# Windowed attention with sinks, then a multiplicative FFN: two megabytes of weights uncast by SyncE, sink scores in column tiles, sink values by small DMAs

## The chip, the cores and the metric

The kernel runs on one core of one Trainium2 chip. The metric is the device time of one execution in microseconds (us). Kernels that are compared ran in turn on the same chip. A run counts as slow when it is over 1.5% above the fastest of the same kernel; 10 of the 47 runs of the kernel before beside e1 to e15, and two of e11, are slow. The medians below are of all runs, the ratios of the fast ones alone. Engine names are those of the profile: PE is TensorE, PEld its weight loads, DVE VectorE, ACT ScalarE, POOL GpSimd, SP SyncE; "SPq" marks what SyncE's queue issues. L-numbers are lines of the kernel that was profiled, so the same statement has other numbers in another kernel.

The kernel before is itself uneven. In 18 of those 47 runs its mean granted clock was 0.983 to 0.991, and these took 210.04 us or more; the other 29 (0.995 to 1.000) took 207.32 to 210.10 us. The profiled run is one of the latter, so no trace shows where the clock falls in the former.

A ratio below is the mean time of one kernel's fast runs over the mean of the other kernel's fast runs of the same rounds. It is therefore not quite the ratio of the medians that stand beside it.

## The reference, cut to what matters

```python
def _attn_ref(q, k, v, n_sink, window):       # B, H, S, D = 4, 8, 768, 64; n_sink 4, window 128
    scores = scale * np.matmul(q, k.transpose(0, 1, 3, 2))
    keep = is_sink | in_window                # the first 4 keys, or the last 128
    scores = np.where(keep, scores, -1000000000.0)
    a = softmax(scores)                       # [cut: written out with max, exp and sum]
    return np.matmul(a, v)

def _moe_ref(x, w1, w2, w3, w_out):           # 3072 tokens, d_model 512, d_ff 1024
    h = (x @ w1) * (x @ w2) @ w3
    return h @ w_out
```

## The kernel before

1. **The order of instructions is planned when the kernel is built.** A small list scheduler inside the kernel holds tasks with guessed stage times. It simulates PE, ACT, DVE and SP and emits each engine's instructions in the order that this simulation gives. On the chip each engine follows its list in order, however the true times fall.
2. **Loads** of q, k, v and most weights are cast from float32 to bfloat16 on the way, by DMAs that GpSimd issues. The first half of w_out (1 MB) comes uncast by SyncE and is cast by ScalarE.
3. **w3 and w_out are folded** into w3 x w_out at the start, while q, k and v arrive.
4. **Batches 2 and 3 get their q and k transposed by DMA**, issued by SyncE: 12 a batch. SyncE also issues the 24 output stores.
5. **The output buffer** `o_sb` has three copies. ScalarE fills one from PSUM, SyncE stores it, and only then may ScalarE fill it again.

```python
    work = ctx.enter_context(tc.tile_pool(name="work", bufs=3))
    ps_mm = ctx.enter_context(tc.tile_pool(name="ps_mm", bufs=4, space=PSUM))
    # ...
    def transposes_dma(src, dst, kb):                     # batches 2 and 3
        nc.sync.dma_start_transpose(out=dst[:, :, kb * P:(kb + 1) * P], in_=src[:, kb, :])
        yield
    # ...
    def sink_values(b):                                   # 8 matmuls and a copy
        vp = ps_mm.tile([P, H, D], FP32, tag="mm", name="vp")
        for h in range(H):
            nc.tensor.matmul(vp[:, h, :], sel[:, h, :], vN[b][:, 0, h, 0:D],
                             start=(h == 0), stop=(h == H - 1))
        yield
        nc.scalar.copy(vs[b][:, :, 0:D], vp[:])
        yield

    def sink_scores(b, t):                                # 4 full-width matmuls, summed
        sp = ps_mm.tile([P, 256], FP32, tag="mm", name="sp")
        for r in range(NP):
            nc.tensor.matmul(sp[:], ksbd[b][:, r * P:(r + 1) * P],
                             qT[b][:, r, t * 256:(t + 1) * 256],
                             start=(r == 0), stop=(r == NP - 1))
        yield
        nc.scalar.activation(es[b][:, (t - 1) * 256:t * 256], sp[:], ACTF.Exp, scale=scale)
        yield
    # ...
    def project(b, m):
        po = ps_mm.tile([P, DM], FP32, tag="mm", name="po")
        # ... 8 matmuls
        yield
        o_sb = work.tile([P, DM], FP32, tag="o_sb", name="o_sb")      # 3 buffers
        nc.scalar.copy(o_sb[:], po[:])
        yield
        nc.sync.dma_start(out=out[t0:t0 + P, :], in_=o_sb[:])
        yield
```

The softmax here doesn't subtract the row's maximum and nothing guards it: scores larger than these inputs give would overflow.

## Time and profile before

| | before |
|---|---|
| median of the first 3 runs | 208.65 us (207.53 to 210.79) |
| span of the profiled run | 207.3 us |
| PE busy | 196.6 us, 95% |
| filler matmuls ("pz", meant only to keep PE's clock up) | 8.66 us, all before 15 us |
| longest wait of PE after the start | 2.51 us, ending at 94.58 us |

The page of the kernel before: the busy line, then three rows of the picture in 40 slices of 5.2 us (busy tenths of PE and ACT, granted PE clock in tenths; 9 is 90% or more).

```profile
PE 196.6 (95%) x1841; PEld 124.6 (60%) x1853; DVE 109.9 (53%) x262; ACT 112.6 (54%) x191; POOL 75.5 (36%) x98
PE   7999799999999999977999999999999999999992
ACT  4204567637657876665686766677654333333331
PEclk9999999999999999999999999999999999999999
```

PE is full nearly everywhere, so PE time is what counts. The dip in the middle is one wait. In the timeline of PE before, the columns are start and length in us, engine, line, operation, operands and count; the bracket gives the idle time ahead and what ended it.

```profile
94.58 0.41 PE L207 MATMUL vp<-vN_93,sel 128*128 128x64 bf16 x8 [2.51 <-DMA vN_93<-in_v_dram]
97.25 1.05 PE L217 MATMUL sp<-qT_96,ksbd_112 128*128 128x256 bf16 x8
98.13 0.39 PE L284 MATMUL xt<-ident,xn 128*128 128x128 bf16 x4
```

The first line is the wait: PE's list has the sink values of batch 3 next, and their v has not landed. The second line is two groups of sink scores. From 97.25 to the next start at 98.13 they take 0.88 us of the stream, 0.44 us a group.

Timeline of SP before, in the stretch where batch 2 is transposed:

```profile
61.74 0.36 SPq L352 DMA_DIRECT2D out_dram<-o_sb  x1
63.09 1.30 SPq L192 DMA_TRANSPOSE kT_100<-kN_88  x1
64.50 1.98 SPq L192 DMA_TRANSPOSE qT_96<-qN_84  x1
66.53 1.29 SPq L192 DMA_TRANSPOSE kT_100<-kN_88  x1
67.87 0.59 SPq L352 DMA_DIRECT2D out_dram<-o_sb  x1
68.51 1.26 SPq L192 DMA_TRANSPOSE qT_96<-qN_84  x1
...
87.20 1.32 SPq L192 DMA_TRANSPOSE qT_96<-qN_84  x1
```

SyncE counts as idle on a page, as issuing is not busy time. But from 63.1 to 69.8 us its queue has no gap to speak of: each transpose holds it for 1.2 to 2 us, and lands about 8.1 us after its issue.

### The profile page before, as it was taken

How to read it: one execution, taken by the hardware profiler on the slowest of the kernel's cores; microseconds unless marked ns; L12 is line 12 of the kernel's file. 1: busy time of each engine (PE TensorE's matmuls, PEld its weight loads, DVE VectorE, ACT ScalarE, POOL GpSimd, SP SyncE). 2: the span in 40 equal slices, each digit the busy share in tenths (PEclk: the TensorE clock that was granted, in tenths of full speed). 3: DMA queues.
4: the chain of work that ended last, by engine and by line, in shares of the span. 5: the costliest groups of instructions: out<-in, count | busy, mean ns of one | idle time of the engine just before them, and what ended most of it. 6: DMA issues, size and time to landing. Idle time of an engine off the chain costs nothing.

```text
span 207.3 us, 4572 instructions
## 1 busy us (share of the span) xinstructions
PE 196.6 (95%) x1841; PEld 124.6 (60%) x1853; DVE 109.9 (53%) x262; ACT 112.6 (54%) x191; POOL 75.5 (36%) x98
## 2 busy tenths in 40 slices
PE   7999799999999999977999999999999999999992
PEld 2454566797877875645666666666655566654440
DVE  7223586865887684574777757677751144430000
ACT  4204567637657876665686766677654333333331
POOL 7859784499999636652910000000000000000000
PEclk9999999999999999999999999999999999999999
DMA  6999999999999999999999930000004300003332
GB/s 213 152 209 161 182 175 207 185 157 154 155 155 183 137 161 155 127 210 184 145 134 124 153 118 0 5 0 3 0 0 155 152 0 2 3 0 153 151 152 102
DMA packets 96245, 24.94 MB, mean 120 GB/s; under 512 B 88544, under 2 KB 92128, under 8 KB 96224
## 3 DMA queue, kind: packets, MB, share of 16 engines
q0 software_dynamic: 79168, 14.16, 89.9%
q1 hardware_dynamic: 17056, 10.49, 24.3%
q8 instruction: 14, 0.23, 0.5%
q14 instruction: 7, 0.06, 0.1%
HBM read 29.36 MB, written 6.29 MB: 172 GB/s over the span
## 4 chain that ended last, share of the span: by engine, by line
PE 52%; DMA 27%; POOL 16%; issue 3%; ACT 0%; POOLq 0%; ACTq 0%
PE pg L299 27%; PE po L345 16%; DMA w_sb<-in_moe_w_dram 15%; DMA vN_93<-in_v_dram 7%; DMA qN_84<-in_q_dram 6%; PE av L268 4%; PE sc L237 3%; POOL qN_83 L103 3%; POOL vN_91 L103 2%; POOL kN_87 L103 2%; PE xt L284 2%; POOL w_sb L110 1%; POOL qN_84 L103 1%; POOL vN_92 L103 1%; POOL kN_88 L103 1%
## 5 line engine op out<-in xcount | busy, mean ns | idle before, releaser
L299 PEld LDWEIGHTS <-w_sb 128*128 128x128 bf16 x576 | 53.0, 98 | 24.8 <-issue 1.4
L242 ACT ACTIVATE ex<-sc 128x1024 bf16<-128x1024 f32 (+1 forms) x48 | 45.3, 958 | 7.9 <-PE sc L237 6.7
L306 ACT COPY a_sb<-pg 128x384 f32<-128x384 f32 (+1 forms) x72 | 32.0, 445 | 31.9 <-PE pg L299 17.4
L246 DVE TENSOR_TENSOR am<-ex,maskt 128x1024 bf16<-128x1024 bf16 (+1 forms) x48 | 30.3, 642 | 5.5 <-ACT ex L242 5.1
L349 ACT COPY o_sb<-po 128x512 f32<-128x512 f32 x24 | 14.0, 585 | 26.3 <-PE po L345 25.3
L299 PE MATMUL pg<-xT_102,w_sb 128*128 128x256 bf16 x192 | 24.7, 273 | 0.5 <-DMA w_sb<-in_moe_w_dram 0.5
L299 PE MATMUL pg<-xT_103,w_sb 128*128 128x384 bf16 x128 | 23.6, 326 | 0.0
L299 PE MATMUL pg<-xT_104,w_sb 128*128 128x384 bf16 x128 | 23.4, 326 | 0.0
L274 DVE TENSOR_TENSOR xn<-av,rec 128x256 bf16<-128x256 f32 x48 | 20.4, 424 | 1.7
L299 PE MATMUL pg<-xT_105,w_sb 128*128 128x384 bf16 x128 | 21.0, 326 | 0.0
L303 DVE TENSOR_TENSOR ab_109<-a_sb,pg 128x384 bf16<-128x384 f32 x16 | 8.9, 554 | 19.0 <-PE pg L299 19.0
L268 PEld LDWEIGHTS <-am 128*128 128x128 bf16 x352 | 17.0, 97 | 3.1 <-issue 0.3
L272 DVE RECIPROCAL rec<-av 128x4 f32<-128x4 f32 x48 | 8.6, 180 | 17.7 <-PE av L268 17.5
L303 DVE TENSOR_TENSOR ab_106<-a_sb,pg 128x256 bf16<-128x256 f32 x24 | 10.0, 417 | 6.3 <-PE pg L299 5.6
L303 DVE TENSOR_TENSOR ab_107<-a_sb,pg 128x384 bf16<-128x384 f32 x16 | 8.9, 554 | 5.0 <-PE pg L299 3.9
L345 PE MATMUL po<-w3o,ab_106 128*128 128x512 bf16 x44 | 11.0, 379 | 0.2
L345 PE MATMUL po<-w3o,ab_107 128*128 128x512 bf16 x46 | 10.9, 379 | 0.1
L345 PE MATMUL po<-w3o,ab_108 128*128 128x512 bf16 x47 | 10.6, 379 | 0.1
L345 PE MATMUL po<-w3o,ab_109 128*128 128x512 bf16 x47 | 10.5, 379 | 0.1
L303 DVE TENSOR_TENSOR ab_108<-a_sb,pg 128x384 bf16<-128x384 f32 x16 | 8.9, 554 | 2.9 <-PE pg L299 2.1
L334 PEld LDWEIGHTS <-w3t 128*128 128x128 bf16 x64 | 5.8, 97 | 7.4 <-DVE w3t L320 1.2
L359 PE MATMUL pz<-ksbd_113 128*128 128x512 bf16 x29 | 8.7, 452 | 1.3 <-DVE ksbd_113 L142 1.3
(142 smaller groups left out, 273.8 us busy)
## 6 DMA issues: line engine op xcount, KB each, us to landing
out_dram<-o_sb SPq DMA_DIRECT2D x24, 256.0 KB, 2.0
w_sb<-in_moe_w_dram POOLq DMA_DIRECT2D x5, 512.0 KB, 11.5
w_sb<-in_moe_w_dram POOLq DMA_DIRECT2D x6, 256.0 KB, 7.8
ab_107<-in_moe_w_out_dram SPq DMA_DIRECT2D x2, 512.0 KB, 3.7
kN_86<-in_k_dram POOLq DMA_DIRECT2D x6, 128.0 KB, 11.4
qN_82<-in_q_dram POOLq DMA_DIRECT2D x6, 128.0 KB, 11.2
vN_90<-in_v_dram POOLq DMA_DIRECT2D x6, 128.0 KB, 9.9
kN_87<-in_k_dram POOLq DMA_DIRECT2D x6, 128.0 KB, 6.6
```

What stands on the lines that cost most here:

```text
L103: nc.gpsimd.dma_start(out=dst, in_=rows(src, b, kb))
L242: nc.scalar.activation(ex[:, :, c0:], sc[:, :, c0:], ACTF.Exp, scale=scale)
L246: nc.vector.tensor_mul(am[:, :, c0:], ex[:, :, c0:], mk)
L268: nc.tensor.matmul(o, lhs, rhs, start=(n == 0), stop=(n == len(todo) - 1), skip_group_check=True)
L272: nc.vector.reciprocal(rec[:], av[:, :, :, D:D + 1])
L274: nc.vector.tensor_mul(xn[:], av[:, :, :, 0:D], rec[:].to_broadcast([P, 2, 2, D]))
L299: nc.tensor.matmul(pg[:], w_sb[:, kk, dt * P:(dt + 1) * P], xT[b][:, kk, tk], start=(kk == 0), stop=(kk == NP - 1))
L303: nc.vector.tensor_mul(ab[b][:, dt, tk], gate_a.pop((b, c, dt))[:], pg[:])
L306: nc.scalar.copy(a_sb[:], pg[:])
L345: nc.tensor.matmul(po[:], ab[b][:, kk, m * P:(m + 1) * P], w3o[:, kk, :], start=(kk == 0), stop=(kk == KFF - 1))
L349: nc.scalar.copy(o_sb[:], po[:])
L359: nc.tensor.matmul(pz[:], idle[:, 0:P], idle[:, 0:512], start=True, stop=True)
```

## The change

The intent: begin the fold sooner by bringing twice as many weight bytes on the uncast path, which starts earlier; let the four sink-score matmuls of a group, whose outputs lie in four separate strips of 32 partitions, run side by side; and take the sink values off TensorE and ScalarE by copying them with eight small DMAs a batch (4 rows of 128 bytes each).

```diff
-    EARLY = 8
+    EARLY = 7
-    order = [('w3', 2, 4, 1, 2), ('w3', 0, 2, 0, 1), ('w3', 2, 4, 0, 1), ('wo', 1), ...
+    order = [('w3', 0, 2, 1, 2), ('wo', 1), ('w3', 2, 4, 1, 2), ('w3', 5, 6, 0, 2), ...   # cut
-    for k0 in (0, 2):                        # 2 x 512 KB of w_out by SyncE, cast by ScalarE
-        nc.sync.dma_start(out=raw[:, k0:k0 + 2, :], in_=moe_w_out[...])
-        nc.scalar.copy(wo_sb[:, k0:k0 + 2, :], raw[:, k0:k0 + 2, :])
+    casts = [load_raw(w3_sb, moe_w3, 0, raw(0, 0)), load_raw(wo_sb, moe_w_out, 0, raw(1, 0)),
+             load_raw(wo_sb, moe_w_out, 2, raw(1, 1)), load_raw(w3_sb, moe_w3, 2, raw(0, 1))]
+    nc.vector.tensor_copy(*casts[0])
+    for x in casts[1:]:
+        nc.scalar.copy(*x)
@@ sink values (sel and its building are removed; vs is set to zero first)
-            nc.tensor.matmul(vp[:, h, :], sel[:, h, :], vN[b][:, 0, h, 0:D], ...)
-        nc.scalar.copy(vs[b][:, :, 0:D], vp[:])
+            m = 32 * (h // 2) + 4 * (h % 2)
+            nc.sync.dma_start(out=vs[b][m:m + 4, h, 0:D], in_=vN[b][0:4, 0, h, 0:D])
@@ sink scores
-            nc.tensor.matmul(sp[:], ksbd[b][:, r * P:(r + 1) * P], qT[...],
-                             start=(r == 0), stop=(r == NP - 1))
+            rows = slice(32 * r, 32 * r + 32)
+            nc.tensor.matmul(sp[rows, :], ksbd[b][:, r * P + 32 * r:r * P + 32 * r + 32],
+                             qT[...], start=True, stop=True)
@@ guesses of the planner
-    clock = 4.0            # first cast load
+    clock = 6.5
-                        clock += 0.75      # a load that is transposed by DMA
+                        clock += 1.05
+    SP_US = 0.7            # was 0.1 for a store
-    task(("sv", b), 2, sink_values(b), [("pe", 0.3), ("act", 0.5)], ...)
+    task(("sv", b), 2, sink_values(b), [("sp", 8 * SP_US), ("dma", 4.0)], [], [("v", b, 0)])
-    task(("ss", b, t), 2, sink_scores(b, t), [("pe", 0.5), ("act", 0.4)], ...)
+    task(("ss", b, t), 2, sink_scores(b, t), [("pe", 0.25), ("act", 0.4)], ...)
```

More of the change, by code (lines that the diff above doesn't have):

```diff
@@ L68 @@
     maskt = const.tile([P, 2, 512], BF16, name="maskt")
-    sel = const.tile([P, H, P], BF16, name="sel")
     ones_s = const.tile([P, H], BF16, name="ones_s")
@@ L125, in load, with raw, load_raw @@
             load_w(dst, src, i[0] * 512, (i[0] + 1) * 512)
-    order = [('w3', 2, 4, 1, 2), ('w3', 0, 2, 0, 1), ('w3', 2, 4, 0, 1), ('wo', 1), ('w3', 0, 2, 1, 2),
-             ('w3', 6, 8, 0, 2), ('qkv', 0, 0, 2), ('w3', 4, 5, 0, 2), ('w3', 5, 6, 0, 2), ('qkv', 0, 2, 4),
-             ('w1', 0), ('w2', 0), ('w2', 1), ('w1', 1), ('qkv', 0, 4, 6), ('qkv', 1, 0, 6),
-             ('qkv', 2, 0, 6), ('qkv', 3, 0, 6)]
+    order = [('w3', 0, 2, 1, 2), ('wo', 1), ('w3', 2, 4, 1, 2), ('w3', 5, 6, 0, 2), ('qkv', 0, 0, 2),
+             ('w3', 6, 8, 0, 2), ('qkv', 0, 2, 4), ('w3', 4, 5, 0, 2), ('w2', 0), ('w1', 0), ('w1', 1),
+             ('w2', 1), ('qkv', 0, 4, 6), ('qkv', 1, 0, 6), ('qkv', 2, 0, 6), ('qkv', 3, 0, 6)]
     nc.scalar.preload_act_table_set("natural_log_exp_and_others")
-    raw = ab[1][:].rearrange("p k s -> p (k s)")[:, 0:4 * DM * 2].bitcast(FP32).rearrange(
-        "p (k n) -> p k n", n=DM)
-    for k0 in (0, 2):
-        nc.sync.dma_start(out=raw[:, k0:k0 + 2, :],
-                          in_=moe_w_out[k0 * P:(k0 + 2) * P, :].rearrange("(ko ki) n -> ki ko n", ki=P))
-        nc.scalar.copy(wo_sb[:, k0:k0 + 2, :], raw[:, k0:k0 + 2, :])
+    def raw(b, i):
+        return ab[b][:].rearrange("p k s -> p (k s)")[:, i * 2048:(i + 1) * 2048].bitcast(FP32).rearrange(
+            "p (k n) -> p k n", n=512)
+    def load_raw(dst, src, i0, tile_):
+        nc.sync.dma_start(out=tile_, in_=src[i0 * P:(i0 + 2) * P, 0:512].rearrange("(ko ki) n -> ki ko n", ki=P))
+        return dst[:, i0:i0 + 2, 0:512], tile_
+    casts = [load_raw(w3_sb, moe_w3, 0, raw(0, 0)), load_raw(wo_sb, moe_w_out, 0, raw(1, 0)),
+             load_raw(wo_sb, moe_w_out, 2, raw(1, 1)), load_raw(w3_sb, moe_w3, 2, raw(0, 1))]
     idle = ksbd[B - 1]
@@ L156 @@
     nc.vector.memset(maskt[0:4, 0, P:3 * P], 1.0)
-    nc.vector.memset(sel[:], 0.0)
-    nc.vector.memset(sel[0:4, :, :], 1.0)
-    sel4 = sel[0:4].rearrange("p (r e) m -> p r e m", e=2)
-    nc.gpsimd.affine_select(sel4, sel4, compare_op=ALU.is_equal, fill=0.0, base=0,
-                            pattern=[[-32, NP], [-4, 2], [1, P]], channel_multiplier=-1)
     nc.vector.memset(ones_s[:], 1.0)
@@ L174 @@
             nc.vector.memset(ksbd[b][:], 0.0)
+        nc.vector.memset(vs[b][:], 0.0)
         nc.vector.tensor_copy(vs[b][:, :, D], ones_s[:])
@@ L203, in sink_values @@
     def sink_values(b):
-        vp = ps_mm.tile([P, H, D], FP32, tag="mm", name="vp")
         for h in range(H):
-            nc.tensor.matmul(vp[:, h, :], sel[:, h, :], vN[b][:, 0, h, 0:D],
-                             start=(h == 0), stop=(h == H - 1))
-        yield
-        nc.scalar.copy(vs[b][:, :, 0:D], vp[:])
+            m = 32 * (h // 2) + 4 * (h % 2)
+            nc.sync.dma_start(out=vs[b][m:m + 4, h, 0:D], in_=vN[b][0:4, 0, h, 0:D])
         yield
@@ L216, in sink_scores @@
         for r in range(NP):
-            nc.tensor.matmul(sp[:], ksbd[b][:, r * P:(r + 1) * P],
-                             qT[b][:, r, t * 256:(t + 1) * 256],
-                             start=(r == 0), stop=(r == NP - 1))
+            rows = slice(32 * r, 32 * r + 32)
+            nc.tensor.matmul(sp[rows, :], ksbd[b][:, r * P + 32 * r:r * P + 32 * r + 32],
+                             qT[b][:, r, t * 256:(t + 1) * 256], start=True, stop=True)
         yield
@@ L363 @@
     LAG = 1.5
-    clock = 4.0
+    clock = 6.5
     issue, landed = 1.3, []
-    arrive["wo", 0] = 7.0
+    arrive["w3", 0, 0] = arrive["w3", 1, 0] = 5.4
+    arrive["wo", 0] = 8.0
+    arrive["w3", 2, 0] = arrive["w3", 3, 0] = 9.3
     def lands(us, *keys):
@@ L441 @@
                 task(("sk", b), 0, sink_keys(b), [("dve", 0.2)], [("sc", b, 1, 0)])
-                task(("sv", b), 2, sink_values(b), [("pe", 0.3), ("act", 0.5)],
-                     [("av", b - 2, NP - 1, NT - 1)] if b >= 2 else [], [("v", b, 0)], "mm")
+                task(("sv", b), 2, sink_values(b), [("sp", 8 * SP_US), ("dma", 4.0)], [], [("v", b, 0)])
             else:
-                task(("ss", b, t), 2, sink_scores(b, t), [("pe", 0.5), ("act", 0.4)],
+                task(("ss", b, t), 2, sink_scores(b, t), [("pe", 0.25), ("act", 0.4)],
                      qk + [("sk", b)], ring="mm")
@@ L484 @@
             for m in range(t0 // P, t1 // P):
-                task(("p", b, m), 1300 + 200 * b + m, project(b, m), [("pe", 1.75), ("act", 0.6), ("sp", 0.1)],
+                task(("p", b, m), 1300 + 200 * b + m, project(b, m), [("pe", 1.75), ("act", 0.6), ("sp", SP_US)],
                      [("g", b, c, KFF - 1, 1), *[("fm", i, 1 if i < SPLIT else 0) for i in range(KFF)]], ring="mm")
```

## The prediction

> **What bounds the kernel now.** TensorE. The page's busy line gives PE 95% of 207.3 us, and the chain of waits runs on PE unbroken from 94.58 to 203.38 us; a tail (last eviction and store) of 3.9 us follows. Before that the chain is loads. PE's lost time, from the timeline and the busy-by-window table: no useful matmul until 8.48 us, where the first w3 rows land (filler matmuls "pz": 8.66 us in all); about 1 us at 20 to 25 us (w3 rows); 0.5 us at 40.5 us (last gate weight); 2.51 us at 92.1 to 94.6 us, where PE stands in order at the sink-value matmuls "vp" of batch 3 while v has not landed, though gate matmuls of batch 1 follow directly. ACT (54%) and DVE (53%) have slack.
>
> **What the change does, costed.**
> 1. vp is removed. Its eight matmuls occupy 0.23 us of the stream a batch (22.18 to 22.41 us): 0.9 us of PE in all, plus four ACT copies of 0.59 us off the chain. 32 small SyncE DMAs replace it. Stores cost SyncE about 0.5 us each to issue, transposes 1.2 to 1.3 us, so I estimate 4 to 6 us of SyncE per batch plus a few to land. For batch 0 that ends near 29 us; the first use was at 34.88 us. For batches 2 and 3 they sit between DMA transposes (8.1 us to landing); mostly hidden.
> 2. The 2.51 us stall goes, since PE no longer reads v there. I credit 2 us.
> 3. Sink scores: two groups take 0.88 us of the stream (97.25 to 98.13 us), four full-width 256-column matmuls each. As four 32-column tiles they should overlap. The Trainium skill, "TensorE: Matmul & The Clock Gate", Part 3, gives 2.38x for three column tiles; "TensorEngine Tiling (Array Packing)", Key Properties, says that changing tiling mode drains the array. No run here shows either yet. Estimate 0.22 us a group instead of 0.44: 8 x 0.22 = 1.8 us of PE.
> 4. Front: 2 MB instead of 1 MB come by SyncE, whose first 512 KB landed by 4.16 us, against 8.3 us for the first cast load. First w3 transposes near 5.5 us. But bytes are conserved: 6.5 MB of source landed by 21 us, about 330 GB/s, so w1 and w2 will be complete at about 40 us as now, and the first q, k, v near 19.5 us instead of 21. The fold needs w_out as well. Of three earlier microseconds I credit only 1.3. The casts (1.04 us each on ACT) run while those engines idle; mask building on POOL comes later and may delay the first masked tile slightly.
>
> Sum: 0.9 + 2.0 + 1.8 + 1.3 = 6.0 us; less 1 us for new waits = 5.0 us. Steps 1 and 3 lie wholly on the chain, as PE is saturated.
>
> **Prediction: 203.6 us, range 200.0 to 207.0** (8 in 10). Faster by over 2%: 0.60; within 2%: 0.36; slower: 0.04.
>
> **What would show each step.** Right: no PE wait over 1 us at 85 to 100 us; sp groups of four in 0.15 to 0.25 us; first w3 transpose before 6.5 us and filler below 7.5 us; the same 3.9 us tail. Wrong: sp still 0.4 us a group (column tiles serial); PE idle at av naming the sink-value DMA; transposes of batch 2 or 3 landing later and scores waiting; gates waiting for w1 or w2 after 35 us (front gain given back to loads).
>
> **What would make it wrong.** SyncE's in-order queue holding transposes behind sink values; the small DMAs taking 10 us under the cast stream; SyncE's large loads delaying the cast loads by more than they save; tile-mode drains eating step 3; or a tighter plan than I credit, giving 200 us.

## The result, and the profile after

The changed kernel took 215.12 us (median of 4, 214.81 to 215.57) against 209.72 us before (median of 4 in the same comparison). The ratio is 1.0339 with a 95% interval of 1.0281 to 1.0398: it is slower by 3.4%, and the prediction of 203.6 us was wrong in direction.

The same lines of the page after:

```profile
PE 196.1 (92%) x1824; PEld 122.9 (57%) x1824; DVE 110.8 (52%) x265; ACT 111.1 (52%) x188; POOL 73.2 (34%) x95
PE   7869799999999999219999999999999999999992
ACT  2323357736738766034677767687756433332331
PEclk9999999999999999956999999999999999999999
```

There is a hole in PE (2, 1) at slices 17 and 18, ACT stands still in the same place (0, 3), and the granted clock there is 5 and 6 tenths. The rest of PE's row and of the clock's looks much as before. The timeline of PE after has one long wait from 30 us to the end:

```profile
67.24 0.40 PE L215 MATMUL sp<-qT_94,ksbd_110 128*32 128x256 bf16 x8
67.58 0.40 PE L281 MATMUL xt<-ident,xn 128*128 128x128 bf16 x4
95.23 0.59 PE L281 MATMUL xt<-ident,xn 128*128 128x128 bf16 x4 [8.47 <-ACT o_sb L346]
```

The first two lines show that the column tiles work: two groups in a row now take 0.34 us (67.24 to 67.58), 0.17 us each. (A group that stands alone takes 0.22 to 0.23 us, as at 33.87 and 48.79 us.) The third is the loss: 8.47 us in which PE waited for ScalarE's copy into `o_sb`. ScalarE in turn, in its own timeline:

```profile
94.59 0.59 ACT L346 COPY o_sb<-po 128x512 f32<-128x512 f32 x1 [10.69 <-DMA out_dram<-o_sb]
```

It stood for 10.69 us because all three output buffers were taken. The chain of waits says why. Its columns are start, length and what:

```profile
67.53 8.08 DMA qT_95<-qN_83
...
75.63 0.58 SPq L207
...
87.04 7.47 DMA out_dram<-o_sb
...
94.59 0.59 ACT o_sb L346
```

And SyncE's queue in that stretch:

```profile
66.91 0.52 SPq L349 DMA_DIRECT2D out_dram<-o_sb  x1
67.53 1.31 SPq L192 DMA_TRANSPOSE qT_95<-qN_83  x1
68.94 7.27 SPq L207 DMA_DIRECT2D vs_115<-vN_91  x8
76.31 1.20 SPq L192 DMA_TRANSPOSE kT_99<-kN_87  x1
77.61 2.48 SPq L192 DMA_TRANSPOSE qT_95<-qN_83  x1
...
85.57 1.39 SPq L192 DMA_TRANSPOSE qT_95<-qN_83  x1
87.04 0.53 SPq L349 DMA_DIRECT2D out_dram<-o_sb  x1
```

The third output store was ready at 67.94 us (its copy began at 67.35 us and takes 0.59 us). It was issued at 87.04 us, behind eight small DMAs and six transposes, and landed 7.47 us later. That landing is long, but not unusual for this stretch, by the semaphore records of the traces. The 24 stores of the kernel before land in 2.0 us at the median, but those that it issued among transposes at 67.87, 83.70, 86.30 and 88.62 us took 6.80 to 7.50 us. In run e13 below, which has no small DMAs there, the same store took 7.10 us (78.38 to 85.48). What was late was the issue. The sixth copy needs the buffer of the third, and so ScalarE and then PE stop.

The eight small DMAs hold the queue for 7.27 us. About 5 us of that is issue (eight for batch 1, with no transpose in flight, took 5.00 us from first to last). Most of the rest, 1.7 us, is a wait of the eighth: in the built program each of these DMAs waits for the completion semaphore of the one issued eight before it, and for the eighth that one was a transpose, issued at 67.53 us and landed at 75.61 us. Excerpt of the built program's list for SyncE (not a profile):

```
22 L192 DmaTransposeAnt qT_95<-qN_83 128x4x128 [waits DMAHW7_49,DMASW1_49,DVE_49]
23 L207 DMACopy vs_115<-vN_91 4x64 [waits DMAHW0_49,DMASW6_49]
...
30 L207 DMACopy vs_115<-vN_91 4x64 [waits DMAHW7_49]
```

The hole costs more than its length. Busy time of PE by stretch after, with the granted clock as the column PEclk (behind POOL):

```profile
core 0: us, PE busy (x) PEld busy (x) DVE busy (x) ACT busy (x) POOL busy (x), PEclk, DMA share, GB/s
86.76:95.23 8.47, 0.00 (x2) 0.00 (x0) 0.00 (x0) 0.64 (x2) 3.56 (x5) 0.69 1.73 157
95.23:100.23 5.00, 5.00 (x27) 2.98 (x27) 1.85 (x4) 3.14 (x5) 1.75 (x2) 0.50 1.74 224
100.23:105.23 5.00, 5.00 (x48) 3.04 (x47) 3.59 (x8) 3.16 (x6) 0.88 (x1) 0.99 1.63 173
```

For 5 us after the hole PE ran at half clock: 27 matmuls in 5 us, then 48 (of mixed kinds). The Trainium skill, "TensorE: Matmul & The Clock Gate", Part 1, says that TensorE falls to half rate after at least one idle window of about 3.4 us and comes back after at least one busy window of that length. This trace agrees: the clock was 0.50 from 90.04 us, 3.28 us after PE stopped, to 100.28 us, 5.05 us after PE went on. Five microseconds at half clock are an estimated 2.5 us of lost work. Together with the hole that is 11 us, while the kernel lost only 5.4 us, so something was gained elsewhere.

**Theory A**: SyncE's in-order queue is the new limit. Eight small DMAs ahead of transposes and stores hold it, and what they hold up stops PE. **Rival B**: the small transfers, or the larger SyncE loads, slow the data itself. **Rival C**: the new front (2 MB uncast and the new order) costs the time.

### The profile page after: what moved, and what is told of

Same layout as the page of the kernel before. It is cut to its first block, busy times and chain, and to the rows that moved or that the text cites. A ratio compares the mean times of both kernels' runs of the same rounds, so it can differ in the third digit from the quotient of the medians.

```text
span 213.9 us, 4584 instructions
## 1 busy us (share of the span) xinstructions
PE 196.1 (92%) x1824; PEld 122.9 (57%) x1824; DVE 110.8 (52%) x265; ACT 111.1 (52%) x188; POOL 73.2 (34%) x95
## 4 chain that ended last, share of the span: by engine, by line
PE 72%; DMA 13%; SPq 5%; POOL 5%; ACT 2%; issue 1%; DVE 1%; POOLq 0%; ACTq 0%
PE pg L296 37%; PE po L342 16%; DMA w_sb<-in_moe_w_dram 6%; PE av L265 6%; SPq L192 5%; PE sc L234 5%; DMA qT_95<-qN_83 4%; DMA out_dram<-o_sb 3%; PE pw L331 3%; PE xt L281 2%; PE tp L183 2%; POOL w_sb L109 1%; POOL kN_85 L102 1%; POOL vN_89 L102 1%; POOL qN_81 L102 1%
## 5 line engine op out<-in xcount | busy, mean ns | idle before, releaser
L296 PE MATMUL pg<-xT_102,w_sb 128*128 128x384 bf16 x128 | 26.1, 346 | 0.0
L296 PE MATMUL pg<-xT_103,w_sb 128*128 128x384 bf16 x128 | 24.1, 326 | 0.0
L271 DVE TENSOR_TENSOR xn<-av,rec 128x256 bf16<-128x256 f32 x48 | 20.4, 425 | 1.7
L296 PE MATMUL pg<-xT_104,w_sb 128*128 128x384 bf16 x128 | 21.0, 326 | 0.0
L265 PEld LDWEIGHTS <-am 128*128 128x128 bf16 x352 | 17.5, 98 | 3.5 <-issue 0.3
L281 PE MATMUL xt<-ident,xn 128*128 128x128 bf16 x96 | 9.5, 223 | 8.5 <-ACT o_sb L346 8.5
L281 PEld LDWEIGHTS <-xn 128*128 128x128 bf16 x96 | 7.1, 99 | 11.7 <-issue 8.9
L342 PE MATMUL po<-w3o,ab_105 128*128 128x512 bf16 x48 | 11.3, 379 | 0.0
L342 PE MATMUL po<-w3o,ab_106 128*128 128x512 bf16 x48 | 11.3, 379 | 0.0
L342 PE MATMUL po<-w3o,ab_107 128*128 128x512 bf16 x48 | 10.7, 379 | 0.0
```

Source lines behind the costliest of these rows:

```text
L265: nc.tensor.matmul(o, lhs, rhs, start=(n == 0), stop=(n == len(todo) - 1), skip_group_check=True)
L271: nc.vector.tensor_mul(xn[:], av[:, :, :, 0:D], rec[:].to_broadcast([P, 2, 2, D]))
L281: nc.tensor.transpose(xt[:, r, i, :], xn[:, i, :, :].rearrange("p e d -> p (e d)"), ident[:])
L296: nc.tensor.matmul(pg[:], w_sb[:, kk, dt * P:(dt + 1) * P], xT[b][:, kk, tk], start=(kk == 0), stop=(kk == NP - 1))
L342: nc.tensor.matmul(po[:], ab[b][:, kk, m * P:(m + 1) * P], w3o[:, kk, :], start=(kk == 0), stop=(kk == KFF - 1))
```

## The experiments

Every kernel was planned anew by its own scheduler unless it says that the order is the same. The four runs e13 to e15 and e1 keep the changed kernel's order on the engines that matter, and weigh most. e3 keeps it too, but for the engine that issues the stores. "Before" in each comparison is the kernel before, on the same chip in the same rounds.

| run | edit, from which kernel | time, us | ratio to before (95%) | longest PE wait after 60 us |
|---|---|---|---|---|
| the change | | 215.12 | 1.0339 (1.028 to 1.040) | 8.47 us |
| e1 | change, four output buffers | 212.57 | 1.016 (1.010 to 1.022) | 5.40 us |
| e2 | change, sink values by matmul | 208.45 | 0.996 (0.990 to 1.002) | 1.53 us |
| e3 | change, stores by ScalarE | 226.15 | 1.080 (1.075 to 1.086) | 15.37 us |
| e4 | before, column tiles only | 209.59 | 1.001 (0.994 to 1.008) | 4.29 us |
| e5 | before, front only | 208.06 | 0.998 (0.993 to 1.003) | none over 0.25 us |
| e6 | before, sink DMAs only | 215.63 | 1.035 (1.028 to 1.042) | 7.73 us |
| e7 | change, sink DMAs for batches 0, 1 | 206.89 | 0.992 (0.985 to 1.000) | none over 0.25 us |
| e8 | before, column tiles and 1.05 | 207.76 | 0.997 (0.990 to 1.003) | 2.08 us |
| e9 | e7 with the old front | 206.67 | 0.994 (0.988 to 1.000) | 1.30 us |
| e10 | change, sink DMAs of 2, 3 late | 205.65 | 0.987 (0.981 to 0.994) | 0.60 us |
| e11 | e10 with the old front | 206.82 | 0.985 (0.978 to 0.993) | 1.68 us |
| e12 | e10 with wide sink scores | 206.72 | 0.988 (0.982 to 0.994) | 0.54 us |
| e13 | change, same order, no sink DMA for 2, 3 | 204.71 | 0.980 (0.974 to 0.985) | none over 0.25 us |
| e14 | change, same order, half of them | 206.56 | 0.990 (0.983 to 0.997) | 1.16 us |
| e15 | e13, same order, wide sink scores | 206.11 | 0.986 (0.981 to 0.991) | none over 0.25 us |

All runs gave correct results except e13, e14 and e15, which leave sink values at zero. Some further kernels did not build: six output buffers, or four together with the matmul path, need more SBUF than is left.

### e1: one more output buffer, same order

```diff
-        o_sb = work.tile([P, DM], FP32, tag="o_sb", name="o_sb")
+        o_sb = work.tile([P, DM], FP32, tag="o_sb", bufs=4, name="o_sb")
```

> The changed kernel with four output buffers instead of three; every engine's instructions stand in exactly the same order. Theory A (one output store is held on SyncE's in-order queue behind eight sink-value DMAs and six transposes, its buffer blocks ScalarE, ScalarE blocks TensorE for 8.5 us, and 5 us of half clock follow, costing some 2.5 us more): the stall at 86.8 to 95.2 us and the low clock vanish, and the time falls by 9 to 11 us to 204 to 206 us. Rival B (the small DMAs or the SyncE loads slow the transfers themselves): the stall moves by less than 3 us to another wait and the time stays above 211 us.

Measured: 212.57 us. Theory A's number failed; the time is above 211 us, as rival B said. But the wait for the output buffer is gone, as theory A says, and a new wait stands 7 us later, not under 3 us (timeline of PE, e1):

```profile
102.57 0.40 PE L215 MATMUL sp<-qT,ksbd 128*32 128x256 bf16 x4 [5.40 <-DMA qT<-qN]
```

This is the next thing behind the same queue: transposes of batch 2 that SyncE could issue only at 93.82 us (its last), where the kernel before issued its last at 87.20 us. So the first form of theory A, "one held store", was too narrow. What is late is everything that SyncE issues after the small DMAs.

### e2: sink values by matmul again

```diff
+    sel = const.tile([P, H, P], BF16, name="sel")        # and its building, as before
-            nc.sync.dma_start(out=vs[b][m:m + 4, h, 0:D], in_=vN[b][0:4, 0, h, 0:D])
+            nc.tensor.matmul(vp[:, h, :], sel[:, h, :], vN[b][:, 0, h, 0:D], ...)
+        nc.scalar.copy(vs[b][:, :, 0:D], vp[:])
```

> The changed kernel with sink values by matmul and ScalarE copy as before; the planner plans again. Theory A: without the eight small DMAs the store is issued in time; no stall over 3 us, time 203 to 207 us. If the front of the change (2 MB uncast) is what costs, the time stays above 211 us.

Measured: 208.45 us, no hole. The whole loss leaves with the small DMAs, which speaks against C. It was 1.5 us above the expected range; with `sel` built where the changed order puts it, PE also waited 1.86 us for it at 24.59 us, a fault of this hybrid.

### e3: output stores issued by ScalarE

```diff
-        nc.sync.dma_start(out=out[t0:t0 + P, :], in_=o_sb[:])
+        nc.scalar.dma_start(out=out[t0:t0 + P, :], in_=o_sb[:])
```

> The changed kernel with the output stores issued by ScalarE, so that they do not stand behind sink-value DMAs and transposes. Theory A: the stall goes, about 204 to 207 us (each store costs ScalarE about half a microsecond, hidden except in the tail). Rival B: no gain, above 211 us.

Measured: 226.15 us, far worse. That is on rival B's side of the numbers (above 211 us), but the trace shows another reason. The waits of e3 (who waits for what: us in total, times, longest) and the timeline of PE:

```profile
ACT o_sb L346 <- DMA qT<-qN: 20.4, 1, 20.4
82.55 0.89 PE L215 MATMUL sp<-qT,ksbd 128*32 128x256 bf16 x8 [15.37 <-ACT o_sb L346]
```

ScalarE now issues the store, and stood 20.4 us for a transpose. In the built program the stores on ScalarE take their completion semaphores from the same set of eight as SyncE's DMAs, so a store has to wait for whichever transpose used its semaphore last. Moving the store to another engine moved the hold onto the busier engine. The trace fits: ScalarE issued its held store at 81.48 us, 0.07 us after the transpose that used the same semaphore had landed (81.41 us). A store with a semaphore of its own was not tested.

### e4: column tiles alone

```diff
-            nc.tensor.matmul(sp[:], ksbd[b][:, r * P:(r + 1) * P], ...
+            nc.tensor.matmul(sp[rows, :], ksbd[b][:, r * P + 32 * r:r * P + 32 * r + 32], ...
```

> The kernel before with only the sink scores in column tiles. The groups took 0.17 us instead of 0.44 us in the changed kernel's trace: 8 x 0.27 = 2.2 us of TensorE less. If TensorE is the limit as read, 1.5 to 2.5 us faster than before (ratio 0.988 to 0.993); if the gain is off the critical path, ratio 1.00.

Measured: 209.59 us, no gain. The wait at the sink values of batch 3 grew (timeline of PE, e4):

```profile
96.02 0.41 PE L207 MATMUL vp<-vN,sel 128*128 128x64 bf16 x8 [4.29 <-DMA vN<-in_v_dram]
```

PE came to this point with more work behind it and waited longer for the same v: 4.29 us instead of 2.51. After the longer wait the granted clock was 0.50 from 97.00 to 100.42 us, an estimated 1.7 us of lost work; after the 2.51 us it had stayed at 1.00. Three of e4's four runs have a mean clock of 0.990 to 0.992 (209.46 to 210.88 us), the fourth 0.998 (208.22 us). What PE saves ahead of a wait for a load is given back at that wait.

### e5 and e6: the other two parts alone

e5 takes only the front from the change, e6 only the sink DMAs with the planner's numbers for them.

> The kernel before with only the new front (2 MB uncast by SyncE, new load order, new casts, the planner's arrival times for them). By the prediction's step 4: 1.3 us faster. By the reading of the changed trace, where TensorE had 3.0 us less useful work behind it at 40 us (25.3 against 28.3 us of non-filler busy time): 1 to 3 us slower, if nothing later hides it; ratio 1.005 to 1.015.

> The kernel before with only the sink values by 32 small SyncE DMAs (with the planner's SyncE and transpose times that came with them). If the small DMAs are the cause of the slowdown (SyncE's queue is held among DMA transposes, TensorE then waits on a held store or on transposes of batch 2), this alone is 5 to 9 us slower than before and shows a TensorE stall of over 4 us between 80 and 110 us. If the front is the cause, ratio 0.99 to 1.01.

Measured: e5 208.06 us (ratio 0.998, no difference), e6 215.63 us (ratio 1.035). e6 is the whole slowdown of the change, with the same signature (timeline of PE, e6):

```profile
92.39 0.58 PE L275 MATMUL xt<-ident,xn 128*128 128x128 bf16 x4 [7.73 <-ACT o_sb L340]
```

Rival C falls as the cause of the loss: by e5's interval the front costs at most 0.3%. The interval reaches down to 0.993, so the predicted gain of 1.3 us (0.6%) is neither shown nor excluded. e5 shows one thing more. PE had 14.57 us of non-filler work by 30 us (23.00 less 8.43), 4.0 us less than in the kernel before, and after that no wait of 0.25 us: even the sink values of batch 3, by matmul as before, began at 93.90 us without one. What PE did later at the start, it did not have to wait for afterwards.

### e7: small DMAs only where there are no transposes

The sink values of batches 0 and 1 come by small DMAs, those of 2 and 3 by matmul (`if b >= 2:` around the old code).

> The changed kernel with small DMAs for batches 0 and 1 only, which have no DMA transposes, and the matmul path for batches 2 and 3. If what costs is the small DMAs among the transposes and not the small DMAs as such: no TensorE stall over 4 us after 60 us, 206.5 to 209 us, like the run with matmuls for all four. If small DMAs cost as such: about half way, 211 to 212 us.

Measured: 206.89 us, and PE has no wait of 0.25 us after 30 us. Sixteen small DMAs show no cost where SyncE has nothing else to do. It is their company that costs.

### e8: column tiles with a later planned arrival

```diff
-                        clock += 0.75
+                        clock += 1.05
```

> The kernel before with column tiles and with the planner's allowance for a transposed load at 1.05 us instead of 0.75 us, nothing else. With column tiles alone the wait for v of batch 3 grew from 2.5 to 4.3 us and ate the gain. If that wait is only a planning error, a later planned arrival lets gate matmuls go ahead of it: stall below 1.5 us, 204 to 206.5 us, faster than both kernels. If TensorE had no other ready work there, the time stays at 208 to 210 us.

Measured: 207.76 us, a wait of 2.08 us for v at 96.35 us. The expected size failed: the time lies between the two cases. A better guess halves the wait of e4 but does not remove it.

### e9: the old front under e7

e7 with `order`, the uncast loads, the casts and their planned arrivals as before.

> The run with small DMAs for batches 0 and 1 only, with the old front put back (1 MB uncast, old load order, old planned arrivals); column tiles and the later planned arrivals kept. That run had 3.7 us less non-filler TensorE time by 30 us than the kernel before (14.85 against 18.56), and no stall afterwards. If TensorE is then the only limit, the old front gives that back: 201 to 203.5 us. If the stream of loads decides when batches 2 and 3 can be worked on, a wait for loads reappears near 95 us and the time is 205 to 208 us. Either way faster than, or level with, the kernel before.

Measured: 206.67 us. PE had 18.18 us of non-filler work by 30 us (27.82 less 9.64), 3.3 us more than e7, and gained nothing: waits for loads came back (1.30 us for v at 95.05 us, and 28.80 us busy instead of 30 between 30 and 60 us). So a faster or slower front shows no difference here: what PE gains early it waits for later, at loads, the last of these waits being at 95 us.

### e10: all small DMAs, but behind the transposes

```diff
-                task(("sv", b), 2, sink_values(b), [("sp", 8 * SP_US), ("dma", 4.0)], [], [("v", b, 0)])
+                task(("sv", b), 2, sink_values(b), [("sp", 8 * SP_US), ("dma", 4.0)],
+                     [(f"tp{x}", b, kb) for x in "kq" for kb in range(2, NB)] if b >= 2 else [], [("v", b, 0)])
```

> The changed kernel with all 32 small DMAs, but those of batches 2 and 3 may be planned only when the transposes of that batch are planned to have landed, so they stand behind them on SyncE. If their place in the queue (ahead of transposes and stores) is what costs: no stall of TensorE over 4 us, 206 to 210 us. If eight small DMAs among transposes cost wherever they stand: over 212 us.

Measured: 205.65 us, ratio 0.987. All 32 small DMAs are there and the change is now 1.3% faster than the kernel before (below the 2% that counts as a clear difference, but the interval excludes 1). In SyncE's timeline of e10 those of batch 2 stand after its transposes and no longer hold them or the early stores, though they take even longer:

```profile
96.48 1.22 SPq L192 DMA_TRANSPOSE kT<-kN  x1
97.75 8.50 SPq L207 DMA_DIRECT2D vs<-vN  x8
```

It is the place in the queue. The late place is not free either: PE's longest wait after 60 us, 0.60 us at 107.81 us, is for these small DMAs, and so are e11's 1.68 us and e12's 0.54 us. With e11 and e12, which cannot be told from it, this is the best correct version that was run.

### e11 and e12: front and column tiles under e10

> The run with late small DMAs (204.0 us span, no stall of 1 us after 30 us), with the old front put back. By 30 us the new front had 14.98 us of non-filler TensorE time (25.51 less 10.53), the kernel before 18.56. If TensorE is now the only limit: 3 to 4 us faster than that run, 201.5 to 203 us. If the loads of batches 1 to 3 set the pace between 40 and 100 us, waits for loads eat it: 204.5 to 207 us.

> The run with late small DMAs, with sink scores full width again. Column tiles alone on the kernel before gained nothing, as a wait for a load grew instead. Here TensorE has no such wait, so if their 8 x 0.27 us are real, this run is 1.5 to 2.5 us slower than the run with late small DMAs: 207 to 208.5 us, ratio near 1.00 to the kernel before. If column tiles are worth nothing even on a busy TensorE: 205 to 206.5 us.

Measured: e11 206.82 us (0.985), e12 206.72 us (0.988). Against e10 (0.987, in other rounds) neither shows a difference that these intervals could resolve. e11's upper case failed, as with e9. For the column tiles this was inconclusive, and e15 asked again in one order.

### e13, e14 and e15: the changed kernel's own order

e13 leaves out the small DMAs of batches 2 and 3, e14 keeps four of eight, e15 is e13 with the sink-score matmuls full width. PE, ACT, DVE and POOL keep the changed kernel's order (in e15 two neighbouring loads of GpSimd have changed places).

```diff
-        for h in range(H):
+        for h in range(H if b < 2 else 0):      # e13, e15; 4 instead of 0 in e14
```

> The changed kernel in exactly its own order on every engine, but the 16 small DMAs of batches 2 and 3 are left out (the sink values of these batches stay zero: wrong on purpose). No planning differs, so this isolates the DMAs' own cost. If they hold SyncE and nothing else is wrong: the 8.5 us stall and the low clock go, 203.5 to 206.5 us. If the plan itself (front, order) is at fault: a stall of over 4 us elsewhere, above 210 us.

> As the run before, but four of the eight small DMAs are kept for each of batches 2 and 3 (heads 4 to 7 stay zero: wrong on purpose). The eight took 7.3 us of SyncE in batch 2, of which 1.7 us was the wait for a transpose issued eight DMAs earlier; four should take about 2.5 us and never wait for it. If the hold is what counts, the stall is far below half, under 3 us, and the time 204 to 209 us; if the number of DMAs alone counts, about half of the loss, 209 to 211 us.

> As the run without the 16 small DMAs, same order again, with sink scores full width (wrong on purpose in the same way). Against that run: 8 x 0.27 = 2.2 us slower if TensorE is the limit all through, 1.5 to 2.5 us; under 0.7 us if waits for loads absorb it.

Measured: 204.71, 206.56 and 206.11 us. Without the 16 DMAs the same order has no hole at all. SyncE in e13, then in e14, in the stretch shown above:

```profile
67.66 1.30 SPq L192 DMA_TRANSPOSE qT<-qN  x1
69.05 1.56 SPq L192 DMA_TRANSPOSE kT<-kN  x1
...
78.38 0.53 SPq L349 DMA_DIRECT2D out_dram<-o_sb  x1
```

```profile
67.11 1.31 SPq L192 DMA_TRANSPOSE qT<-qN  x1
68.51 2.59 SPq L207 DMA_DIRECT2D vs<-vN  x4
71.20 1.20 SPq L192 DMA_TRANSPOSE kT<-kN  x1
...
80.69 0.54 SPq L349 DMA_DIRECT2D out_dram<-o_sb  x1
```

And the ScalarE copy that needs the third buffer, in e13, then in e14:

```profile
85.56 0.58 ACT L346 COPY o_sb<-po 128x512 f32<-128x512 f32 x1 [1.43 <-DMA out_dram<-o_sb]
```

```profile
87.47 0.58 ACT L346 COPY o_sb<-po 128x512 f32<-128x512 f32 x1 [3.38 <-DMA out_dram<-o_sb]
```

The third store leaves at 78.38 us with none, at 80.69 us with four, at 87.04 us with eight. ScalarE waits for the buffer for 1.43, 3.38 and 10.69 us, and PE for 0, 1.16 and 8.47 us. Rival B is not needed: the store lands 7.10 us after its issue without the small DMAs and 7.47 us with eight. The cost is not in proportion to the number: four cost 1.9 us (206.56 less 204.71), eight 10.4 us (215.12 less 204.71, across two comparisons whose kernel before was alike, 209.54 and 209.72 us). A hold of 2.59 us is nearly taken up by the three output buffers; one of 7.27 us is not, it stops ScalarE and PE; and after a stop of 8.47 us the clock falls as well.

e15 less e13 is 1.40 us, just under the 1.5 to 2.5 us expected: the worth of the column tiles when PE waits for nothing. The traces show why it is not 8 x 0.27 = 2.2 us. The 0.17 us hold only where two groups stand together, and PE sometimes takes longer to go over to the tiles. Counted from the start of the matmul before a stretch of tiles to the start of the one after it, the eight groups (six stretches) take 2.67 us in e13 and 4.43 us in e15, so 1.76 us less.

## Why the prediction was wrong

The bound was read rightly: PE was full before and is full in the good variants. The terms, one by one:

- **Step 1, sink values, "mostly hidden": this is the step that failed.** I put 4 to 6 us of SyncE a batch between transposes that each take 1.2 to 2 us of the same queue and land 8 us later, and charged for it 1 us in all ("less 1 us for new waits"). The eight held the queue for 7.27 us in batch 2, and 16 of them cost 10.4 us (e13). The estimate of the hold was somewhat low (7.27 us, and 6.15 us in batch 3). That was not the failure. What I did not do was ask what stood behind it: a store whose buffer ScalarE needs, and ScalarE's PSUM copies that PE needs. Of the dangers listed, the first ("SyncE's in-order queue holding transposes behind sink values") was the right one. Its first victim, however, was a store, and transposes only when that was mended (e1).
- **Step 2, the 2.51 us wait.** It is gone in e13, which has no wait of 0.25 us after 30 us. But it is gone in e5 and e7 too, where PE still reads this v (at 93.90 and 94.98 us). So it is not shown that it went because PE no longer reads v there. In the changed kernel the hole stood in its place.
- **Step 3, column tiles.** The tiles overlap: 0.17 us a group in a pair instead of 0.44, and 0.22 to 0.23 us for a group alone, as estimated. In time they are worth 1.40 us (e15), not 1.8, and nothing while a wait for a load follows (e4).
- **Step 4, the front, credited 1.3 us.** It gave nothing clear (e5, ratio 0.998, interval 0.993 to 1.003). The first w3 transpose did start sooner, at 6.88 us instead of 8.48, though not before 6.5 us, and the filler grew to 9.23 us instead of falling below 7.5. And PE had less non-filler work done by 30 us (24.54 less 9.23, so 15.31 us, against 27.22 less 8.66, so 18.56 us): the second w_out piece was cast only at 11.06 us and the second w3 piece at 13.81 us, and PE waited for both. This did not matter in the end, since later waits for loads level it out (e9).

Without the small DMAs of step 1 the sum nearly holds: e13 is 4.3 us faster than before (2.04% of 209.54 us, with an interval on both sides of 2%), where the prediction said 5.0. That is partly luck. Of it, 1.4 us are the column tiles. The other 2.9 us happen to be the 2.0 and 0.9 predicted for the wait and the matmuls of the sink values, but by subtraction alone: the front and the uneven clock of the kernel before are in them, and no run separates these.

What stays open: whether a front that is faster under the same loads could help once loads of batches 1 to 3 come sooner, how much of e3's 20.4 us is due to shared semaphores alone, and what moving the 16 small DMAs would do if every other engine kept its order (e10 was planned anew).

## What to carry to other kernels

A queue that only issues DMAs looks idle in a profile, but it is an engine with an order: before adding work to it, read its timeline, and ask for each item behind the new work when it is needed and who holds a buffer until then. Work saved on a full engine counts only up to the next wait for a load. If a change is slower, keep its parts and try their place in the order: here the change with all its 32 DMAs was 3.4% slower than the kernel before with them in one place, and 1.3% faster with them in another.

## What the Trainium skill lacked or had wrong

- "DMA: Bandwidth & Descriptors", Issuing engines are not separate DMA queues, says that initiating a DMA takes the sequencer a time that is usually small relative to the DMA itself. That held for one small DMA (0.58 us of SyncE, 5.0 to 5.7 us to landing in batch 1). What the section lacks is that these times add up on one queue: eight took 5.00 us with nothing in the way, and 16, issued ahead of transposes and stores, cost the kernel 10.4 us.
- I found no page with the issue and landing time of a DMA transpose of 128 x 512 bf16 from SBUF to SBUF (the same page has cycles per instruction for other shapes): 1.2 to 2.6 us of SyncE and about 8.1 us to landing in these runs.
- No page says that the built program gives its SyncE and ScalarE DMAs eight completion semaphores in turn, so that each waits for the one eight before. Here one small DMA waited until a transpose landed at 75.61 us, and ScalarE, which issued the stores in e3, waited 20.4 us.
- "TensorEngine Tiling (Array Packing)", Theoretical Speedup, gives up to 4 times for 32 columns and, under Key Properties, a drain at each change of tiling mode, without a time for it. Eight groups of four 32-column tiles with 256 moving columns took 2.67 us (e13) instead of 4.43 us at full width (e15), 1.7 times, with the ways in and out included. In three of the six stretches the first tile began 0.09 us later after the matmul before it than at full width.
- "TensorE: Matmul & The Clock Gate", Part 1, was borne out in the rate, 0.50 in each case, but not in every time: it asks for an idle window of about 3.4 us. The clock fell 3.28 us after PE stopped in the changed kernel and 3.57 us in e1, but after only 2.11 us in e6; in e4 it fell 5.27 us after PE stopped, when PE had already worked again for 0.98 us. It came back 4.4 to 5.1 us after PE went on (e4, e6, e1 and the change).
